# Hash-masked attention and gated feed-forward: the score scale moved into the query rows, and the exponential's factor and shift instructions removed

## The chip, the cores and the metric

The kernel runs on one core of a Trainium2 chip. The metric is the device time of one execution in microseconds, the median over runs. The engines are named as the profile names them: PE (matrix multiply, with PEld for its weight loads), DVE (vector), ACT (scalar, activation functions), POOL (GpSimd) and SP (whose queue issues almost all DMAs).

## The reference

The reference is an attention in which a query row sees only the keys that fall into the same hash bucket, followed by a gated feed-forward layer. Sizes: 4 batches, 8 heads, 768 positions, head size 64, 6 hash bits; all arithmetic is in float32.

```
q_bits = (einsum('bhsd,dk->bhsk', q, proj) > 0);  k_bits likewise
mask   = q_bucket[:, :, :, None] == k_bucket[:, :, None, :]
scores = (1 / sqrt(64)) * q @ k^T
scores = where(mask, scores, -1e9);  scores = scores - max(scores)
attn   = exp(scores);  attn = attn / (sum(attn) + 1e-09)
x      = attn @ v                      # heads side by side: 4 x 768 x 512
gate   = sigmoid(causal depthwise convolution of x, 5 taps)
out    = (gate * (x @ w_val)) @ w_out
```

A query row without any key in its bucket has the same score, -1e9, everywhere, so its weights are 1/768 each.

## The kernel before

There are 32 units (batch, head), and each has 6 tiles of 128 query rows by 768 keys: 192 tiles, numbered k. The queries and keys of a unit arrive transposed in one array `r` of 128 rows, queries in rows 0 to 63 and keys in rows 64 to 127. `prep` makes four operands of it, in a rounded and a remainder part, so that two passes of matmuls (`scores`, L266) give an accurate product: `aq`, `ak` (rounded; 12 further rows carry the hash bits, so that a mismatch adds a large negative number to the score) and `bq`, `bk` (remainders crossed with rounded parts). POOL makes the rounded copy (L170, `aq<-r`) and the remainder (L173, `bq<-r,aq`); six DMAs of SP (L174 to L177, L181, L182) then move the halves to where the matmul needs them, and L148 (`load_raw`) fetches the `r` of five units later. The operands exist twice (`stk`, two buffers), so the operands of unit i+1 are made while unit i is computed.

A tile runs through these steps. PE writes the scores `s` into one of two PSUM buffers. DVE takes the negated row maximum `nm` (L272). `factors` (L278, DVE) makes `gs`, which is the score scale 1/8 for an ordinary row and 0 for a row without a match; `shifts` (L282, DVE) makes `nb = nm * gs`. ACT computes `p = exp(gs * s + nb)` and the row sum (L290). For each pair of tiles, DVE adds 1e-9 to the sums (L296) and takes the reciprocal `ri` (L300); POOL multiplies `p` by it (L305). Three tiles later PE transposes `p` (L314), ACT copies the transposes out of PSUM (L323, `pt<-tp`), and PE multiplies them with the values (L337, `av`). ACT copies `av` to `x` (L345); DVE and POOL do the convolution (L366, L368), ACT the gate (L372), and PE the two feed-forward products (L399, L424). The 8 weight blocks come as 64-bit numbers and are turned into a rounded and a remainder part during the first quarter: a DMA on SP (L137), ACT's absolute value (L91), DVE and POOL operations (L93 to L113).

The order on PE, ACT, DVE and POOL is written out by hand: one loop over k (L490 and on) issues, for each k, the copies of tile k-4, the maximum of k, the sums of the pair before, the normalisation of k-2, `scores(k+1)`, the exponential of k, and one step each of the generators for convolutions, weights, feed-forward, `prep` and `attn_v`. A generator stops at each `yield` and goes on in a later iteration. `prep` of the next unit is created when k is the last tile of a unit (k = 5 modulo 6), gets its first step there and one step per tile after it; `finish(preps)` forces the rest before the first `scores` of the next unit. SP is not ordered by hand: a scheduler places its DMAs by its own estimate of when they become ready.

Of the kernel before, what the change touches and what calls it, by code (L numbers as in the profile page):

```python
# [8 lines left out]
FP32 = mybir.dt.float32  # L9
# [17 lines left out]
def kernel(  # L27
# [13 lines left out]
    D = 64  # L41
# [38 lines left out]
    cw_sb = const.tile([P, NP * KW], FP32, name="cw_sb")  # L80

# [79 lines left out]
    def prep(i):  # L161
# [8 lines left out]
        nc.gpsimd.tensor_copy(out=aq, in_=r)  # L170
        if i > 1:
            yield
        nc.gpsimd.tensor_tensor(out=bq, in0=r, in1=aq.bitcast(FP32), op=ALU.subtract)  # L173
# [64 lines left out]
    def first_prep():  # L238
# [7 lines left out]
        nc.scalar.copy(out=aq[0:D], in_=r[0:D])  # L246
# [3 lines left out]
        for g in (0, 2, 3, 1):  # L250
            if g == 1:
                nc.vector.tensor_tensor(out=bq[D:P], in0=r[0:D], in1=aq[0:D].bitcast(FP32), op=ALU.subtract)  # L252
# [4 lines left out]
        nc.scalar.copy(out=bq[0:D], in_=r[0:D])  # L257
# [11 lines left out]
    def maxima(k):  # L269
        s = ss[k]  # L270
        nm = small.tile([P, 1], FP32, name="nm")
        nc.vector.tensor_reduce(out=nm, in_=s[:, :, 0:HS], axis=AX.XY, op=ALU.max, negate=True)  # L272
        nms[k] = nm

    def factors(k):

        gs[k] = small.tile([P, 1], FP32, name="gs")
        nc.vector.tensor_scalar(out=gs[k], in0=nms[k], scalar1=BIG / 2, scalar2=scale, op0=ALU.is_lt, op1=ALU.mult)  # L278

    def shifts(k):  # L280
        nbs[k] = small.tile([P, 1], FP32, name="nb")
        nc.vector.tensor_scalar(out=nbs[k], in0=nms.pop(k), scalar1=gs[k], scalar2=None, op0=ALU.mult)  # L282

    def exponentials(k):
        s, nb = ss.pop(k), nbs.pop(k)
# [4 lines left out]
        nc.scalar.activation(out=p, in_=s[:, :, 0:HS], func=AF.Exp, bias=nb, scale=gs.pop(k), accum_out=sm[:, k % 2, 0:1])  # L290
        ps[k] = (p.rearrange("p a b -> p (a b)"), sm)


    def row_sums(k):
        sums[k] = small.tile([P, 2, 2], FP32, name="s1")
        nc.vector.tensor_scalar(out=sums[k][:, :, 0], in0=ps[k][1][:, :, 0], scalar1=1e-9, scalar2=None, op0=ALU.add)  # L296

    def recip(k):
        ri = small.tile([P, 2], FP32, name="ri")
        nc.vector.reciprocal(out=ri, in_=sums.pop(k)[:, :, 0])  # L300
        rcs[k], rcs[k + 1] = ri[:, 0:1], ri[:, 1:2]

    def normalise(k):
        p, _ = ps[k]
        nc.gpsimd.tensor_scalar(out=p, in0=p, scalar1=rcs.pop(k), scalar2=1.0, op0=ALU.mult, op1=ALU.mult)  # L305
# [170 lines left out]
    with tc.manual_schedule(engines=ENGINES):  # L476
# [13 lines left out]
        for k in range(N + LAG + 1):  # L490
# [5 lines left out]
            if pair:  # L496
                row_sums(k - 2)
# [100 lines left out]
```

## Time and profile before

| | |
|---|---|
| median of 3 runs | 621.8 us (621.5 to 622.37) |
| profiled execution, span from first to last instruction | 620.8 us |
| PE busy | 585.5 us, 94% of the span |
| DVE busy | 437.6 us, 70% |
| ACT busy | 421.4 us, 68% |
| POOL busy | 395.6 us, 64% |

The profile gives no other time for the profiled execution than its span; the median of the runs lies 1.0 us above it, the lowest run 0.7 and the highest 1.6. Share of busy time is an average over the whole execution: the first third, in which weights are prepared and the operands for later units are loaded, looks different from the rest, and the prediction reads the two apart.

### The profile page before, as it was taken

To read this page: it belongs to the slowest core of one execution; us is meant where nothing else is said; L and a number is where in the kernel's file an instruction comes from. 1 tells how busy PE (TensorE), PEld (TensorE's weight loads), DVE (VectorE), ACT (ScalarE), POOL (GpSimd) and SP (SyncE) were. 2 spreads that over 40 slices of the span, in tenths; PEclk is the share of its full clock that TensorE was granted. 3 is DMA by queue.
4 is the path that set the end of the run, shared out by engine and by line. 5 is a ranking of instruction groups with operands and counts; after the bars stand their busy time and mean duration, and the time that the engine had idled before them with its cause. 6 is when DMAs were issued, how large, how long until landed. Compare 5 with 4: busy or idle time off the path is not lost.

```text
span 620.8 us, 10648 instructions
## 1 busy us (share of the span) xinstructions
PE 585.5 (94%) x3496; PEld 423.4 (68%) x3496; DVE 437.6 (70%) x1017; ACT 421.4 (68%) x881; POOL 395.6 (64%) x373
## 2 busy tenths in 40 slices
PE   5789898989999999999999999999999999999997
PEld 2655565555657777776767777777667877775895
DVE  5869798998975866668575867569665877665532
ACT  2777777778778666777787676777787766765400
POOL 3576868778766765578564777568764777544321
PEclk9799999999999999999999999999999999999999
DMA  6467666564532235243433234333422213200111
GB/s 227 123 197 199 200 167 208 157 175 118 133 83 68 70 79 142 72 108 82 122 82 107 61 80 126 84 115 82 108 70 78 67 42 91 69 18 1 51 52 51
DMA packets 29031, 64.64 MB, mean 104 GB/s; under 512 B 4937, under 2 KB 10057, under 8 KB 28977
## 3 DMA queue, kind: packets, MB, share of 16 engines
q1 hardware_dynamic: 28832, 63.93, 37.8%
q8 instruction: 28, 0.46, 0.3%
q14 instruction: 27, 0.21, 0.1%
q10 hardware_dynamic: 144, 0.03, 0.0%
HBM read 30.60 MB, written 7.86 MB: 62 GB/s over the span
## 4 chain that ended last, share of the span: by engine, by line
PE 66%; DVE 12%; ACT 12%; DMA 5%; issue 3%; POOL 2%; SPq 1%; ACTq 0%; POOLq 0%; DVEq 0%
PE av L337 17%; PE s L266 16%; PE tp L314 12%; PE m L424 8%; PE m L399 7%; ACT p L290 5%; DVE nm L272 4%; ACT pt L323 3%; ACT x L345 2%; DMA w<-in_w_val_dram 2%; DVE g L368 2%; PE tp L399 1%; PE tp L424 1%; PE s L424 1%; DMA bk<-bq 1%
## 5 line engine op out<-in xcount | busy, mean ns | idle before, releaser
L305 POOL TENSOR_SCALAR p<-p,ri 128x768 f32<-128x768 f32 x192 | 210.5, 1100 | 156.0 <-DVE nb L282 130.8
L272 DVE TENSOR_REDUCE nm<-s 128x1 f32<-128x768 f32 x192 | 182.5, 950 | 61.2 <-PE s L266 61.0
L290 ACT ACTIVATE p<-s,nb,gs 128x768 f32<-128x768 f32 x192 | 192.6, 1003 | 46.2 <-DVE nb L282 41.9
L323 ACT COPY pt<-tp 128x384 f32<-128x384 f32 x384 | 165.7, 485 | 75.3 <-PE tp L314 74.4
L314 PEld LDWEIGHTS tp<-ident,p 128*128 128x128 f32 x1152 | 130.3, 142 | 72.2 <-issue 43.6
L314 PE MATMUL tp<-ident,p 128*128 128x128 f32 x1152 | 164.4, 279 | 2.6 <-ACT pt L323 2.1
L337 PE MATMUL av<-pt,vt 128*64 128x384 f32 x768 | 144.9, 498 | 0.0
L266 PE MATMUL s<-ak,aq 76*128 76x384 f32 x384 | 118.1, 389 | 23.2 <-ACT p L290 19.7
L266 PE MATMUL s<-bk,bq 128*128 128x384 f32 x384 | 101.3, 345 | 0.4 <-DVE bq L252 0.4
L337 PEld LDWEIGHTS av<-pt,vt 128*64 128x64 f32 x768 | 47.0, 136 | 61.5 <-issue 61.4
L266 PEld LDWEIGHTS s<-ak,aq 76*128 76x128 f32 x384 | 59.2, 194 | 38.7 <-ACT p L290 34.6
L368 DVE SCALAR_TENSOR_TENSOR g<-x,cw_sb,g 128x768 f32<-128x768 f32 x64 | 79.4, 1241 | 2.2 <-POOL g L366 2.1
L266 PEld LDWEIGHTS s<-bk,bq 128*128 128x128 f32 x384 | 71.7, 194 | 0.8 <-issue 0.8
L173 POOL TENSOR_TENSOR bq<-r,aq 128x768 fp32r<-128x768 f32 x31 | 59.2, 1909 | 0.1
L410 POOL TENSOR_TENSOR hl<-ht,hh 128x384 fp32r<-128x384 f32 x32 | 32.3, 1009 | 39.5 <-DVE hh L408 39.5
L345 ACT COPY x<-av 64x384 f32<-64x384 f32 x64 | 30.4, 475 | 29.7 <-PE av L337 29.0
L282 DVE TENSOR_SCALAR nb<-nm,gs 128x1 f32<-128x1 f32 x192 | 40.4, 211 | 3.5
L399 PE MATMUL m<-xh,wv 128*128 128x384 f32 x200 | 42.7, 337 | 0.0
L358 POOL TENSOR_TENSOR xl<-x,xh 128x384 fp32r<-128x384 f32 x32 | 33.4, 1059 | 13.8 <-DVE xh L357 13.8
L290 ACT ACTIVATION_READ_ACCUMULATOR p<-s,nb,gs 128x1 f32 x192 | 39.0, 203 | 0.0
L404 DVE TENSOR_TENSOR ht<-m,g 128x384 f32<-128x384 f32 x25 | 13.9, 556 | 35.6 <-PE m L399 29.2
L424 PE MATMUL m<-wo,hh 128*128 128x512 f32 x144 | 38.1, 394 | 0.0
(86 smaller groups left out, 486.9 us busy)
## 6 DMA issues: line engine op xcount, KB each, us to landing
r<-in_qk_dram SPq DMA_DIRECT2D x32, 384.0 KB
vt<-in_v_dram SPq DMA_DIRECT2D x16, 384.0 KB
out_dram<-o SPq DMA_DIRECT2D x24, 256.0 KB
ak<-aq SPq DMA_DIRECT2D x31, 192.0 KB
bk<-aq SPq DMA_DIRECT2D x31, 192.0 KB
bk<-bq SPq DMA_DIRECT2D x31, 192.0 KB
bq<-aq SPq DMA_DIRECT2D x31, 192.0 KB
hh<-in_qk_dram SPq DMA_DIRECT2D x16, 192.0 KB
```

The costliest lines, as they stand in the source:

```text
L173: nc.gpsimd.tensor_tensor(out=bq, in0=r, in1=aq.bitcast(FP32), op=ALU.subtract)
L266: nc.tensor.matmul(out=s[:, hf, 0:HS], lhsT=lq[0:n, qs], rhs=rk[0:n, hf * HS:(hf + 1) * HS], start=n == M, stop=n == P)
L272: nc.vector.tensor_reduce(out=nm, in_=s[:, :, 0:HS], axis=AX.XY, op=ALU.max, negate=True)
L290: nc.scalar.activation(out=p, in_=s[:, :, 0:HS], func=AF.Exp, bias=nb, scale=gs.pop(k), accum_out=sm[:, k % 2, 0:1])
L305: nc.gpsimd.tensor_scalar(out=p, in0=p, scalar1=rcs.pop(k), scalar2=1.0, op0=ALU.mult, op1=ALU.mult)
L314: nc.tensor.transpose(out=tp[:, n * P:(n + 1) * P], in_=p[:, kb * P:(kb + 1) * P], identity=ident)
L323: nc.scalar.copy(out=pt[:, :, qo:qo + P], in_=tp[:, 0:HS].rearrange("p (a b) -> p a b", b=P))
L337: nc.tensor.matmul(out=av[s * D:(s + 1) * D, 0:HS], lhsT=vt[:, kb, hh * D:(hh + 1) * D], rhs=pt[kb // 3][:, kb % 3, :], start=(kb == 0), s ...
L345: nc.scalar.copy(out=x[hh * D:(hh + 1) * D, o:o + HS], in_=av[s * D:(s + 1) * D, 0:HS])
L368: nc.vector.scalar_tensor_tensor(out=g, in0=x[:, k:k + S], scalar=w, in1=g, op0=ALU.mult, op1=ALU.add)
L399: nc.tensor.matmul(out=acc[:, 0:HS], lhsT=wv[wi][:, c, j * P:(j + 1) * P], rhs=xs_[(c, o)][xi], start=(m == 0), stop=(m == 11))
L424: nc.tensor.matmul(out=acc, lhsT=hs[(o, j)][hi][:, tb * P:(tb + 1) * P], rhs=wo[wi][:, j, :], start=(m == 0), stop=(m == 11))
```

## The change

The score scale, 1/8, goes into the query rows. For units 2 to 31, `prep` gets a new first step, an activation on ACT that multiplies rows 0 to 63 of `r` by the scale in place; the rounded copy on POOL and the remainder with the DMAs behind it each come one step later than before. For unit 1 the scale is part of the two operations that make `aq` and `bq` (a per-row factor `shrink`), and the remainder is made on DVE; for unit 0 it is part of operations that were there already. The exponential then needs no factor: its scale is 1.0 and its bias is `nm` itself, so `factors` and `shifts` are gone. A row without a match is set right later: `unmatched` makes, once per pair of tiles, `fs`, which holds (1, 768) for such a row and (0, 0) for any other; the row sum becomes `max(sum + 1e-9, fs[1])`, and the normalisation on POOL becomes `max(p, fs[0]) * ri`.

```
         r = raws[i]
         aq, ak, bq, bk = stacks[i] = [...]
-        nc.gpsimd.tensor_copy(out=aq, in_=r)
         if i > 1:
-            yield
-        nc.gpsimd.tensor_tensor(out=bq, in0=r, in1=aq.bitcast(FP32), op=ALU.subtract)
+            nc.scalar.activation(out=r[0:D], in_=r[0:D], func=AF.Copy, scale=scale)
+            yield
+            nc.gpsimd.tensor_copy(out=aq, in_=r)
+            yield
+            nc.gpsimd.tensor_tensor(out=bq, in0=r, in1=aq.bitcast(FP32), op=ALU.subtract)
+        else:
+            nc.gpsimd.tensor_scalar(out=aq, in0=r, scalar1=shrink, scalar2=1.0, op0=ALU.mult, op1=ALU.mult)
+            nc.vector.scalar_tensor_tensor(out=bq, in0=r, scalar=shrink, in1=aq.bitcast(FP32),
+                                           op0=ALU.mult, op1=ALU.subtract)
...
-        nc.vector.tensor_scalar(out=gs[k], in0=nms[k], scalar1=BIG / 2, scalar2=scale, op0=ALU.is_lt, op1=ALU.mult)
-        nc.vector.tensor_scalar(out=nbs[k], in0=nms.pop(k), scalar1=gs[k], scalar2=None, op0=ALU.mult)
...
-        nc.scalar.activation(out=p, in_=s[:, :, 0:HS], func=AF.Exp, bias=nb, scale=gs.pop(k), accum_out=sm[:, k % 2, 0:1])
+        nc.scalar.activation(out=p, in_=s[:, :, 0:HS], func=AF.Exp, bias=nms.pop(k), scale=1.0, accum_out=sm[:, k % 2, 0:1])
...
+    def unmatched(k):
+        fs[k] = small.tile([P, 2, 2], FP32, name="fs")
+        nc.vector.scalar_tensor_tensor(out=fs[k], in0=pairs.pop(k).unsqueeze(2).to_broadcast([P, 2, 2]), scalar=BIG / 2,
+                                       in1=alone, op0=ALU.is_ge, op1=ALU.mult)
     def row_sums(k):
-        nc.vector.tensor_scalar(out=sums[k][:, :, 0], in0=ps[k][1][:, :, 0], scalar1=1e-9, scalar2=None, op0=ALU.add)
+        nc.vector.scalar_tensor_tensor(out=sums[k], in0=ps[k][1][:, :, 0], scalar=1e-9, in1=fs[k][:, :, 1],
+                                       op0=ALU.add, op1=ALU.max)
...
-        nc.gpsimd.tensor_scalar(out=p, in0=p, scalar1=rcs.pop(k), scalar2=1.0, op0=ALU.mult, op1=ALU.mult)
+        nc.gpsimd.tensor_scalar(out=p, in0=p, scalar1=f, scalar2=ri, op0=ALU.max, op1=ALU.mult)
```

How the rows stand now on three engines. First DVE, two consecutive tiles between the fifth and the sixth weight block (`nm`, `gs`, `nb`: the maximum, factor and shift of one tile; `s_1397` and `ri`: sums and reciprocals of the pair before; `g`, `xh`: convolution), of which the second tile is even; before:

```order
L272 TENSOR_REDUCE nm<-s 128x1
L278 TENSOR_SCALAR gs<-nm 128x1
L282 TENSOR_SCALAR nb<-nm,gs 128x1
L368 SCALAR_TENSOR_TENSOR g<-x,cw_sb,g 128x768
L357 CAST xh<-x 128x384 x2
L272 TENSOR_REDUCE nm<-s 128x1
L296 TENSOR_SCALAR s_1397<-sm 128x2
L278 TENSOR_SCALAR gs<-nm 128x1
L300 RECIPROCAL ri<-s_1397 128x2
L282 TENSOR_SCALAR nb<-nm,gs 128x1
```

The same place on DVE now (line numbers are higher by the added lines):

```order
L287 TENSOR_REDUCE nm<-s 128x1
L383 SCALAR_TENSOR_TENSOR g<-x,cw_sb,g 128x768
L372 CAST xh<-x 128x384 x2
L287 TENSOR_REDUCE nm<-s 128x1
L303 SCALAR_TENSOR_TENSOR fs<-nm,alone 128x4
L308 SCALAR_TENSOR_TENSOR s_1289<-sm,fs 128x2
L313 RECIPROCAL ri<-s_1289 128x2
```

An odd tile has lost two small instructions and gained none; an even tile has lost two and gained one, and its three small instructions now form a chain, `fs` to `s` to `ri`.

Next POOL, where the operands of unit 5 are made (`wv`: the end of a weight block); before:

```order
L305 TENSOR_SCALAR p<-p,ri 128x768
L113 TENSOR_TENSOR wv_121<-w_527 128x512
L170 CAST aq<-r 128x768
L305 TENSOR_SCALAR p<-p,ri 128x768
L173 TENSOR_TENSOR bq<-r,aq 128x768
```

Unit 5 on POOL now:

```order
L119 TENSOR_TENSOR wv_127<-w_490 128x512
L320 TENSOR_SCALAR p<-p,fs,ri 128x768
L179 CAST aq<-r 128x768
L320 TENSOR_SCALAR p<-p,fs,ri 128x768
L381 TENSOR_SCALAR g<-x,cw_sb 128x768
L181 TENSOR_TENSOR bq<-r,aq 128x768
```

The copy and the remainder each stand one normalisation later, and here the convolution's first tap (`g`) has come in front of the remainder too; in even-numbered units it has not.

Last SP, the end of the DMAs of unit 6, with the sixth weight block behind them; before:

```order
L176 DMA bk<-bq 64x768
L181 DMA aq<-u 12x768
L154 DMA vt<-in_v_dram 128x768
L177 DMA bq<-aq 64x768
L148 DMA r<-in_qk_dram 128x768
L137 DMA w_1333<-in_w_out_dram 128x1024
```

The same place on SP now:

```order
L188 DMA bk<-bq 64x768
L193 DMA aq<-u 12x768
L154 DMA r<-in_qk_dram 128x768
L189 DMA bq<-aq 64x768
L143 DMA w_1228<-in_w_out_dram 128x1024
```

The weight block still stands behind the whole group, whose first DMA here waits for POOL's remainder; the values (`vt`) have gone ahead of that first DMA.

More of the change, by code (lines that the diff above doesn't have):

```diff
@@ L80 @@
     cw_sb = const.tile([P, NP * KW], FP32, name="cw_sb")
+    shrink = const.tile([P, 1], FP32, name="shrink")
+    nc.gpsimd.memset(shrink[0:D], scale)
+    nc.gpsimd.memset(shrink[D:P], 1.0)
+    alone = const.tile([P, 2, 2], FP32, name="alone")
+    nc.gpsimd.memset(alone[:, :, 0], 1.0)
+    nc.gpsimd.memset(alone[:, :, 1], float(S))
     wv = [const.tile([P, NP, 512], FP32R, name=f"wv{i}") for i in range(2)]
@@ L245, in first_prep @@
                              rhs=r[:, HS * (g % 2):HS * (g % 2 + 1)], start=True, stop=True, tile_position=(0, 32 * g))
-        nc.scalar.copy(out=aq[0:D], in_=r[0:D])
+        nc.scalar.activation(out=aq[0:D], in_=r[0:D], func=AF.Copy, scale=scale)
         nc.vector.tensor_copy(out=bk[D:P], in_=r[D:P])
@@ L251, in first_prep @@
             if g == 1:
-                nc.vector.tensor_tensor(out=bq[D:P], in0=r[0:D], in1=aq[0:D].bitcast(FP32), op=ALU.subtract)
+                nc.vector.scalar_tensor_tensor(out=bq[D:P], in0=r[0:D], scalar=scale, in1=aq[0:D].bitcast(FP32),
+                                               op0=ALU.mult, op1=ALU.subtract)
             nc.vector.tensor_scalar(out=(aq, ak)[g // 2][D:M, HS * (g % 2):HS * (g % 2 + 1)],
@@ L256, in first_prep @@
                                     scalar2=rows_sb[32 * g:32 * g + 2 * NB, 3:4], op0=ALU.is_ge, op1=ALU.mult)
-        nc.scalar.copy(out=bq[0:D], in_=r[0:D])
+        nc.scalar.activation(out=bq[0:D], in_=r[0:D], func=AF.Copy, scale=scale)
     def scores(k):
@@ L270, in maxima @@
         s = ss[k]
[L271 to L282, printed above, removed]
+        if k % 2 == 0:
+            cur["nm"] = small.tile([P, 2], FP32, name="nm")
+        nms[k] = cur["nm"][:, k % 2:k % 2 + 1]
+        nc.vector.tensor_reduce(out=nms[k], in_=s[:, :, 0:HS], axis=AX.XY, op=ALU.max, negate=True)
+        if k % 2:
+            pairs[k - 1] = cur["nm"]
     def exponentials(k):
-        s, nb = ss.pop(k), nbs.pop(k)
+        s = ss.pop(k)
         p = pp.tile([P, 2, HS], FP32, name="p")
@@ L456 @@
     tiles = [(i, qt) for i in range(len(units)) for qt in range(KB)]
-    raws, stacks, vts, ss, nbs, ps, tps, sums, rcs, nms, gs, cur = {}, {}, {}, {}, {}, {}, {}, {}, {}, {}, {}, {}
+    raws, stacks, vts, ss, ps, tps, sums, rcs, nms, pairs, fs, cur = {}, {}, {}, {}, {}, {}, {}, {}, {}, {}, {}, {}
     avs, convs, moes, early = [], [], [], {}
@@ L496 @@
             if pair:
+                unmatched(k - 2)
                 row_sums(k - 2)
-            if k < N:
-                factors(k)
-            if pair:
                 recip(k - 2)
@@ L503 @@
                 normalise(k - 2)
-            if k < N:
-                shifts(k)
             if k + 1 < N:
```

8 lines of the change are left out of this document (5 added, 3 removed).

## The prediction

> **What bounds the kernel now.** I read four views: the busy time of each engine by stage, the waits by stage, the chain of work that ended last, and the groups of instructions. First the page's span and the stages; the columns are the stretch, its length, then the busy time of PE, PEld, DVE, ACT and POOL.
>
> ```profile
> span 620.8 us, 10648 instructions
> 10.00:200.00 190.00, 170.84 (x1054) 111.71 (x1053) 160.01 (x374) 141.75 (x297) 135.64 (x124) 0.98 0.55 150
> 200.00:565.00 365.00, 360.79 (x2180) 269.14 (x2179) 251.28 (x603) 266.75 (x563) 240.22 (x227) 1.00 0.32 84
> ```
>
> From 200 to 565 us PE is busy for 360.8 of 365.0 us: 4.2 us are to be had there, whatever DVE, ACT or POOL save. From 10 to 200 us PE is idle for 19.2 us. That is where the change can pay, and 19.2 + 4.2 = 23.4 us is the most that it can bring there. Next, the waits of the first stage (in total, times, longest), then one of the second:
>
> ```profile
> ACT p L290 <- DVE nb L282: 26.5, 31, 6.0
> PE s L266 <- ACT p L290: 16.9, 24, 1.8
> DVE nm L272 <- PE s L266: 7.3, 9, 1.6
> ACT o L91 <- DMA w<-in_w_val_dram: 3.3, 2, 1.7
> ```
>
> ```profile
> PE s L266 <- ACT p L290: 2.8, 8, 0.4
> ```
>
> In the first stage nearly all of PE's idle time, 16.9 us in 24 waits, is `scores(k+1)` waiting until the exponential of k-1 has freed its PSUM buffer, and ACT in its turn waits for `nb` 31 times, 26.5 us. DVE waits for PE only 7.3 us: it is the engine that sets the pace, and the chain shows how. Columns are start, duration, engine:
>
> ```profile
> 88.63 0.87 DVE nm L272
> ...
> 89.53 0.17 DVE gs L278
> ...
> 89.72 0.21 DVE nb L282
> 89.93 1.28 DVE g L368
> ...
> 91.81 0.87 DVE nm L272
> 92.68 0.07 DVE s L296
> 92.76 0.11 DVE gs L278
> 92.87 0.09 DVE ri L300
> 92.96 0.16 DVE nb L282
> ```
>
> The maximum of an odd tile ends at 89.50 and `nb` at 89.93, so `gs` and `nb` take 0.43 us there; in the even tile the four small instructions take 93.12 - 92.68 = 0.44 us. In both, the exponential and everything behind it on DVE stand behind them.
>
> **The change part by part.** Groups of the whole execution (form, count, busy time, mean ns), and the pairs of tiles in the first stage by the group of their sums there:
>
> ```profile
> L290 ACT ACTIVATE p<-s,nb,gs 128x768 f32<-128x768 f32 x192 | 192.6, 1003 | 46.2 <-DVE nb L282 41.9
> L372 ACT ACTIVATE g<-g 128x768 f32<-128x768 f32 x16 | 12.2, 833 | 0.0
> L246 ACT CAST aq<-r 64x768 fp32r<-64x768 f32 x1 | 0.8, 832 | 1.9 <-DMA r<-in_qk_dram 1.9
> L170 POOL CAST aq<-r 128x768 fp32r<-128x768 f32 x31 | 28.7, 925 | 0.4 <-PE s L266 0.3
> L305 POOL TENSOR_SCALAR p<-p,ri 128x768 f32<-128x768 f32 x192 | 210.5, 1100 | 156.0 <-DVE nb L282 130.8
> L366 POOL TENSOR_SCALAR g<-x,cw_sb 128x768 f32<-128x768 f32 x16 | 15.0, 939 | 0.0
> L296 DVE TENSOR_SCALAR s<-sm 128x2 f32<-128x2 f32 x34 | 5.6, 166 | 1.2 <-ACT p L290 1.2
> ```
>
> *Shorter way from the maximum to the exponential.* Every exponential starts 0.43 to 0.44 us earlier behind its maximum. It also gets shorter: of its two per-row operands (`nb`, `gs`) one is left. The trace has no exponential with one; the bounds are 1003 ns (L290, two) and 833 ns (L372, same shape, none). I take the middle, 0.09 us less. So each of the 24 waits can shrink by 0.44 + 0.09 = 0.53 us, 12.7 us in all. But they average 16.9 / 24 = 0.70 us, some are shorter than 0.53, and some end with something other than `nb`. I take three quarters: **-9.5 us**. From 200 us on only the 0.09 counts, for 8 waits: **-0.7 us**.
>
> The Trainium skill ("ScalarE: Activation LUTs", section "What ACT_TABLE_LOAD costs") says that each per-partition pointer operand of an activation adds about 93 ns. By it the term would be an estimated 0.44 + 0.093 per wait, which moves the sum by less than 0.1 us; no row here shows an activation with just one.
>
> *DVE's own time.* An odd tile loses 0.43 us. An even tile loses `gs` and `nb` and gains `fs`, and `fs`, `s` and `ri` now wait for each other. I count 0.10 for `fs` (its input is old, like the row of `s` above, 0.07) and 0.2 each for `s` and `ri` (like `gs` and `nb` behind the maximum of the odd tile, 0.17 to 0.21 plus a gap of 0.02): 0.5 instead of 0.44. So a pair saves 0.43 - 0.06 = 0.37 us, and the 34 pairs of the first stage 12.6 us. This is the same money seen from the other side, not a further term: it says that 9.5 us can be paid without DVE becoming late again.
>
> *The new step on ACT.* It has the size of L246: 832 ns, for 30 units 25 us. It stands behind the exponential of an odd tile. What covers it later on is this idle time (start, duration, what, idle before):
>
> ```profile
> 312.62 0.19 ACT L290 ACTIVATION_READ_ACCUMULATOR p<-s,nb,gs 128x1 f32 x1
> 313.99 0.86 ACT L323 COPY pt<-tp 128x384 f32<-128x384 f32 x2 [1.19 <-PE tp L314]
> ```
>
> 1.19 us before the next copies hide 0.83 us; without them it would cost 0.83 us per unit. In the first stage, ten units, ACT's wait for `nb` is the cover (26.5 / 31 = 0.85 us each), and the change takes half of that away. Between nothing and 10 x 0.83 = 8.3 us I take **+1.5 us**.
>
> *Later operands.* POOL's remainder now comes behind one more normalisation and the copy: 1.10 + 0.93 = 2.0 us later, and where `g` has slipped in front (about every second unit) another 0.94. Its DMAs move with it. How much room is there? Unit 2 is the tightest that I found (start and duration of the issue; start of the first matmul that reads it; then one such transfer with the releases around it, in another unit):
>
> ```profile
> 33.39 0.48 SPq L177 DMA_DIRECT2D bq<-aq  x1
> 38.66 0.51 PE L266 MATMUL s<-bk,bq 128*128 128x384 f32 x2
> ```
>
> ```profile
> 60.54 2.27 POOL bq L173
> 62.82 2.53 DMA bk<-bq
> 65.37 0.51 SPq L177
> ...
> 66.55 6.39 DMA w<-in_w_val_dram
> ```
>
> A transfer of this size takes 2.53 us; 38.66 - 33.39 - 2.53 = 2.7 us are to spare, and a shift of 2.0 to 2.9 with an earlier next unit uses them up. Most units have more, so I take half a microsecond for three units of the first stage: **+1.5 us** (between 0 and 31 x 0.5 = 15.5).
>
> The same rows hold the weights: the DMA `w` sits on SP behind the whole group, so it too is issued 2 us later, while ACT's L91 stands where it stood. Before, ACT waited like this:
>
> ```profile
> 72.96 0.70 ACT L91 ACTIVATE o<-w 128x512 f32<-128x512 f32 x1 [1.67 <-DMA w<-in_w_val_dram]
> 105.92 0.67 ACT L91 ACTIVATE o<-w 128x512 f32<-128x512 f32 x1 [0.53 <-DMA w<-in_w_out_dram]
> ```
>
> Behind the waiting L91 are queued the copies of transposes and the next exponential, for which PE waits. Three weight blocks (the fourth, sixth and eighth) stand behind such a group: 3 x 2.0 = 6.0 us more of ACT's waiting at most, nothing at least if PE has work meanwhile. I take **+3.5 us**. The second block is now ahead of its group, and its wait (3.3 - 1.67 = 1.6 us) goes; I take about two thirds of that as what PE lost: **-1.0 us**.
>
> *Edits at no cost.* The normalisation with `max` and a second per-row operand: L366 and L305 do 768 numbers with one operand, the copy L170 with none, and the three rows lie between 925 and 1100 ns; POOL has 190 - 136 = 54 us idle in the first stage, so a tenth of a microsecond more on 69 normalisations is hidden; without that cover it would cost 7 us. The constants, unit 0 and unit 1: single instructions at the start, in the cover of the first loads.
>
> The sum: -9.5 - 0.7 - 1.0 + 1.5 + 1.5 + 3.5 = **-4.7 us**, 616.1 us of span. With the 1.0 us between span and median of the runs, 617.1; I say **617.0 us**. A measurement of this kernel can tell about 0.2% (1.2 us) from no change.
>
> **The rivals.**
>
> *All of it lands.* If the DMAs' room suffices and PE works through ACT's waits, only the gains stay: -9.5 - 0.7 - 1.0 = -11.2, 610.6 us. For it: most units have more room than unit 2. Against it: L91 waited already. Chance 0.25.
>
> *The small instructions fight POOL.* `fs` and the new `s` read two tensors from SBUF where `gs`, `nb` and the old `s` read one. The trace shows what that can mean (start, duration):
>
> ```profile
> 311.52 1.04 DVE L368 SCALAR_TENSOR_TENSOR g<-x,cw_sb,g 128x768 f32<-128x768 f32 x1
> 315.54 1.82 POOL L173 TENSOR_TENSOR bq<-r,aq 128x768 fp32r<-128x768 f32 x1
> 316.34 1.84 DVE L368 SCALAR_TENSOR_TENSOR g<-x,cw_sb,g 128x768 f32<-128x768 f32 x1
> 22.38 2.17 POOL L305 TENSOR_SCALAR p<-p,ri 128x768 f32<-128x768 f32 x2 [2.51 <-DVE nb L282]
> 23.69 0.16 DVE L97 SCALAR_TENSOR_TENSOR cw<-cw,cwt 128x20 int32<-128x20 int32 x1
> ```
>
> The same instruction took 1.04 us and, under POOL's remainder, 1.84 us. At that ratio 0.2 us become 0.35, and 2 x 34 of them 10 us, all that the first stage gains: with the costs, 620.8 + 0.5 + 1.0 = 622 us. Against it: L97, a small one of this kind, took 0.16 us while POOL was normalising. Chance 0.05. The Trainium skill says this ("GPSIMD Engine Reference", section "Key points"): POOL shares its SBUF interfaces with the vector engine, and instructions of that engine with two SBUF inputs contend. The L368 rows agree; the L97 row does not show it for a small one.
>
> *The handover becomes the bound.* Slower than before: the operands of each next unit arrive after the first `scores` that needs them. The place is the first `bk,bq` matmul of a unit, the price what the shift (2.0, in every second unit 2.9) exceeds the room by. It decides from (4.7 / 31) = 0.15 us per unit on, beyond what I have counted; at 0.4 us per unit it is 620.8 - 4.7 + 12.4 = 628.5, 629.5 us in the runs, at half that 623. For it: DMAs wait in line on SP, each for the one before. Against it: 2.7 us of room in the tightest unit. Chance 0.15.
>
> *Nothing comes of it.* What is late next on PE's side, the copies of transposes in front of the exponential on ACT, is late by nearly as much: 621.8 us. Chance 0.10.
>
> **How the numbers follow.** The forecast has 0.45, the rivals 0.25, 0.05, 0.15 and 0.10. The first two cases cover 609.5 to 620, from all gains with 1 us of error to the forecast's costs nearly doubled; with the case of no effect and the near end of the slower ones up to 622.5 they hold 0.8. Faster by over 0.2%: 0.45 + 0.25 and 0.03 of the case of no effect, 0.73. Slower: 0.15, and 0.02 each of contention and no effect, 0.19. Within: the rest, 0.08.
>
> **What would show it.** Right: the waits of ACT for the maximum, in the first stage, well under the 26.5 us for `nb`; PE's idle time there down from 19.2 to about 14; the exponential near 910 ns; ACT's waits for `w` longer, two or three of 2 to 4 us. Wrong: an exponential still near 1000 ns; a normalisation well over 1.2 us, which would make POOL the bound; first `scores` of units waiting for DMAs by more than a few tenths; `fs` and `s` over 0.3 us; or a stage after 200 us whose PE idle time grows beyond 4.2 us because the new step on ACT is not covered.

## The result, and the profile after

The change makes the kernel slower: 825.86 us against 622.09 us in the same comparison, a ratio of 1.327 [1.324, 1.329]. The forecast was 617.0 us, faster, with 622.5 as the upper end. First the page of the profiled execution: its span, the busy time of the engines, POOL's share and the granted clock of TensorE in 40 slices, and the chain of work that ended last.

```profile
span 823.9 us, 10497 instructions
PE 650.2 (79%) x3496; PEld 451.7 (55%) x3496; DVE 426.7 (52%) x730; ACT 428.0 (52%) x911; POOL 759.1 (92%) x376
POOL 3999999989999999999999999999999999999521
PEclk9689798878887999998897999999998999998899
POOL 50%; PE 25%; issue 15%; DVE 6%; DMA 2%; ACT 1%; POOLq 0%; DVEq 0%; SPq 0%; ACTq 0%
```

Before, POOL was busy for 395.6 us, PE for 94% of the span. Now POOL is busy for 759.1 us, its row of tenths stands at 9 in all but one slice from the second to the 37th (a 9 is 90% or more), and half of the chain runs through it. DVE and ACT, for whose sake the change was made, hardly differ. The same page says which group it is (busy, mean ns of one, idle before and its releaser):

```profile
L320 POOL TENSOR_SCALAR p<-p,fs,ri 128x768 f32<-128x768 f32 x192 | 581.4, 3034 | 19.0 <-DVE cwt L99 9.4
L329 PE MATMUL tp<-ident,p 128*128 128x128 f32 x1152 | 184.3, 301 | 157.2 <-POOL p L320 154.6
L297 ACT ACTIVATE p<-s,nm 128x768 f32<-128x768 f32 x192 | 175.5, 914 | 23.8 <-DVE nm L287 17.2
```

The normalisation takes 3034 ns where it took 1100. That is 192 x 1.93 = 371 us more work for POOL. Before, POOL was idle for 620.8 - 395.6 = 225 us; now it is idle for 823.9 - 759.1 = 65 us. POOL's busy time grew by 363.5 us in all (its other instructions got a little shorter or fewer); 160 us of that fitted into the idle time, and the other 203 us are what the span grew by. The third line shows that the exponential did become shorter, 914 ns for 1003; the forecast said near 910.

The waits (in total, times, longest) show who stands behind POOL, and the stages (length, then busy PE, PEld, DVE, ACT, POOL; then the granted clock) show that it does so from start to end:

```profile
ACT pt L338 <- PE tp L329: 279.8, 166, 5.1
PEld tp L329 <- POOL p L320: 227.7, 135, 4.0
PE tp L329 <- POOL p L320: 154.6, 100, 3.7
```

```profile
10.00:200.00 190.00, 139.85 (x720) 88.48 (x719) 116.83 (x199) 98.32 (x214) 180.15 (x83) 0.82 0.44 123
200.00:565.00 365.00, 291.94 (x1614) 203.96 (x1614) 182.43 (x317) 206.58 (x441) 359.17 (x173) 0.93 0.27 69
```

The transposes wait for the normalised tile 100 times, 154.6 us, a wait that was not among the large ones before. In the second stage, where PE was busy for 360.8 of 365.0 us, POOL is now, for 359.2. The clock column fell too, to 0.82 and 0.93.

### The profile page after: what moved, and what is told of

Same layout as the page of the kernel before. It is cut to its first block, busy times and chain, and to the rows that moved or that the text cites. A ratio compares the mean times of both kernels' runs of the same rounds, so it can differ in the third digit from the quotient of the medians.

```text
span 823.9 us, 10497 instructions
## 1 busy us (share of the span) xinstructions
PE 650.2 (79%) x3496; PEld 451.7 (55%) x3496; DVE 426.7 (52%) x730; ACT 428.0 (52%) x911; POOL 759.1 (92%) x376
## 4 chain that ended last, share of the span: by engine, by line
POOL 50%; PE 25%; issue 15%; DVE 6%; DMA 2%; ACT 1%; POOLq 0%; DVEq 0%; SPq 0%; ACTq 0%
POOL p L320 34%; PE tp L329 6%; POOL bq L181 6%; PE s L279 5%; PE av L352 4%; POOL xl L373 3%; PE m L439 3%; POOL hl L425 2%; POOL aq L179 2%; DVE nm L287 2%; PE m L414 2%; POOL g L381 1%; PE tp L414 1%; PE tp L439 1%; POOL w L117 1%
## 5 line engine op out<-in xcount | busy, mean ns | idle before, releaser
L320 POOL TENSOR_SCALAR p<-p,fs,ri 128x768 f32<-128x768 f32 x192 | 581.4, 3034 | 19.0 <-DVE cwt L99 9.4
L329 PE MATMUL tp<-ident,p 128*128 128x128 f32 x1152 | 184.3, 301 | 157.2 <-POOL p L320 154.6
L329 PEld LDWEIGHTS tp<-ident,p 128*128 128x128 f32 x1152 | 137.4, 152 | 255.7 <-POOL p L320 227.7
L297 ACT ACTIVATE p<-s,nm 128x768 f32<-128x768 f32 x192 | 175.5, 914 | 23.8 <-DVE nm L287 17.2
L352 PE MATMUL av<-pt,vt 128*64 128x384 f32 x768 | 165.9, 560 | 0.0
L279 PE MATMUL s<-ak,aq 76*128 76x384 f32 x384 | 125.3, 410 | 5.5 <-ACT p L297 3.8
L383 DVE SCALAR_TENSOR_TENSOR g<-x,cw_sb,g 128x768 f32<-128x768 f32 x64 | 87.8, 1372 | 79.2 <-POOL g L381 79.0
L279 PE MATMUL s<-bk,bq 128*128 128x384 f32 x384 | 108.5, 367 | 0.4 <-DVE bq L264 0.4
L297 ACT ACTIVATION_READ_ACCUMULATOR p<-s,nm 128x1 f32 x192 | 39.9, 208 | 0.0
L308 DVE SCALAR_TENSOR_TENSOR s<-sm,fs 128x2 f32<-128x2 f32 x96 | 32.0, 334 | 10.8 <-ACT p L297 1.0
```

Source lines behind the costliest of these rows:

```text
L279: nc.tensor.matmul(out=s[:, hf, 0:HS], lhsT=lq[0:n, qs], rhs=rk[0:n, hf * HS:(hf + 1) * HS], start=n == M, stop=n == P)
L320: nc.gpsimd.tensor_scalar(out=p, in0=p, scalar1=f, scalar2=ri, op0=ALU.max, op1=ALU.mult)
L329: nc.tensor.transpose(out=tp[:, n * P:(n + 1) * P], in_=p[:, kb * P:(kb + 1) * P], identity=ident)
L352: nc.tensor.matmul(out=av[s * D:(s + 1) * D, 0:HS], lhsT=vt[:, kb, hh * D:(hh + 1) * D], rhs=pt[kb // 3][:, kb % 3, :], start=(kb == 0), s ...
L383: nc.vector.scalar_tensor_tensor(out=g, in0=x[:, k:k + S], scalar=w, in1=g, op0=ALU.mult, op1=ALU.add)
```

## Experiments: what made it slower

The theory after the result: one of the two things that are new in the normalisation, `max` or the second per-row operand, is slow on POOL. The rival: the rest of the change, by holding up the tiles, lets POOL's instructions wait inside their own duration.

**The maximum alone.** The kernel before, with one edit:

```
-        nc.gpsimd.tensor_scalar(out=p, in0=p, scalar1=rcs.pop(k), scalar2=1.0, op0=ALU.mult, op1=ALU.mult)
+        nc.gpsimd.tensor_scalar(out=p, in0=p, scalar1=0.0, scalar2=rcs.pop(k), op0=ALU.max, op1=ALU.mult)
```

> The kernel before, with POOL's normalisation as max(p, 0) * ri: the maximum is there, with a constant, and only ri is read per row. If it is the maximum that POOL is slow at, one normalisation takes about 2.9 us as in the changed kernel (1.1 before) and the time is 810 to 840 us. If it is the second per-row operand, the normalisation stays at 1.1 us and the time at 622 us. If only the two together are slow, also 622 us.

808.98 us, ratio 1.297 [1.293, 1.300]. POOL's group:

```profile
L305 POOL TENSOR_SCALAR p<-p,ri 128x768 f32<-128x768 f32 x192 | 564.4, 2946 | 17.3 <-DVE nb L282 16.9 <-PE tp L314 0.4
```

With nothing else changed, a maximum with 0 in the place of a product with 1.0 is worth 186 of the 204 us (808.98 against 622.86 us in this comparison; 810 to 840 was expected). The rest is near what the second operand costs once POOL is the bound, an estimate: (3034 - 2946) x 192 = 17 us.

**The second operand alone.** The kernel before with `p * ri * one`, where `one` is a second per-row operand that holds 1.0.

> The kernel before, with the normalisation as p * ri * one, where one is a column of ones: no maximum, two per-row operands. If the second per-row operand is what is slow, 2.9 us a piece and over 800 us in all; if it is the maximum, 1.0 to 1.2 us a piece and 622 us, within 0.3%.

623.71 us, ratio 1.0008 [0.9993, 1.0024].

```profile
L307 POOL TENSOR_SCALAR p<-p,ri,one 128x768 f32<-128x768 f32 x192 | 227.3, 1187 | 139.7 <-DVE nb L284 118.1 <-PE tp L316 16.3 <-ACT pt L325 2.5
```

1187 ns for 1100: a second per-row operand costs 0.09 us, and here, where POOL has idle time, that is hidden, as the forecast had it.

**The change without the maximum.** The changed kernel with the normalisation of before, `p * ri * 1.0`; everything else is the change.

> The changed kernel with the normalisation as it was before (p * ri, no maximum; left out: the weights of rows without a match, which are then not uniform). This is the rest of the change alone. If the slow normalisation is the whole loss, and the forecast's other terms hold, 617 us (609.5 to 622.5), with the normalisation at 1.1 us. If the later operands or the new step on ACT cost more than forecast, 623 to 630 us. If the loss is not POOL's, over 650 us.

624.88 us, ratio 1.0024 [1.0003, 1.0045].

```profile
L320 POOL TENSOR_SCALAR p<-p,ri 128x768 f32<-128x768 f32 x192 | 202.2, 1057 | 177.0 <-DVE ri L313 96.7 <-PE tp L329 41.3 <-ACT r L177 10.8
```

The normalisation takes 1057 ns. The rest of the change makes nothing slower by much. But it does not make the kernel faster either: +2.0 us where the forecast's sum is -4.7.

**Another way to set the rows right.** The changed kernel with a product and a sum in the normalisation, which gives the same output: `fs` holds (1/768, BIG) for a row without a match, so that `p * ri` is next to nothing there and 1/768 is added.

```
-        nc.gpsimd.tensor_scalar(out=p, in0=p, scalar1=f, scalar2=ri, op0=ALU.max, op1=ALU.mult)
+        nc.gpsimd.tensor_scalar(out=p, in0=p, scalar1=ri, scalar2=f, op0=ALU.mult, op1=ALU.add)
```

> The changed kernel with rows without a match set right by an addition in place of the maximum: p * ri + c, where such a row gets ri near 0 and c = 1/768, any other c = 0. Two per-row operands, two different operations, no maximum. If the maximum is what is slow: the normalisation at 1.0 to 1.2 us and the same time as the kernel without the maximum, within 2 us. If POOL is slow at any pair of different operations, or at two per-row operands, 2.9 us a piece and over 800 us.

626.72 us, ratio 1.0058 [1.0041, 1.0075].

```profile
L320 POOL TENSOR_SCALAR p<-p,ri,fs 128x768 f32<-128x768 f32 x192 | 221.5, 1156 | 160.1 <-DVE ri L313 93.4 <-PE tp L329 32.1 <-DVE cwt L99 8.8
```

The normalisation takes 1156 ns with its two operands. So the idea of the change can be had without the slow operation, at +3.9 us.

**Which operations, and by what they cost.** The kernel before with six forms of the normalisation by turns, all with the same output.

> The kernel before with six forms of the normalisation by turns, one per tile of a unit, all with the same output: a product and a product; a product and a maximum with 0; a minimum with 2 and a product; a sum with 0 and a product; a maximum with 0 and a product on two halves of 384 numbers; the same on 768. If maximum and minimum are slow on GpSimd wherever they stand and by the element: about 2.9 us for the second, third and sixth form, twice 1.5 us for the halves, 1.1 us for the first and fourth. If only a first operation that is no product is slow: 1.1 us for the second, 2.9 us for the fourth. If the cost is one fixed time per instruction: twice 2.5 us for the halves. About 700 us in all.

754.91 us in its one run, where about 700 was expected. The groups, in the order halves with `max` first; `max` first; `mult` then `max`; `min` first; `add` first; two products:

```profile
L315 POOL TENSOR_SCALAR p<-p,ri 128x384 f32<-128x384 f32 x64 | 115.6, 1813 | 31.6 <-DVE nb L282 31.6
L317 POOL TENSOR_SCALAR p<-p,ri 128x768 f32<-128x768 f32 x32 | 94.1, 2939 | 0.0
L307 POOL TENSOR_SCALAR p<-p,ri 128x768 f32<-128x768 f32 x32 | 93.8, 2930 | 0.0
L309 POOL TENSOR_SCALAR p<-p,ri 128x768 f32<-128x768 f32 x32 | 92.8, 2900 | 17.3 <-DVE nb L282 14.8 <-PE tp L328 2.1 <-ACT pt L337 0.4
L311 POOL TENSOR_SCALAR p<-p,ri 128x768 f32<-128x768 f32 x32 | 30.9, 966 | 0.0
L319 POOL TENSOR_SCALAR p<-p,ri 128x768 f32<-128x768 f32 x32 | 29.8, 930 | 7.4 <-DVE nb L282 6.5 <-PE tp L328 0.8
```

Maximum and minimum, first or second, take 2.90 to 2.94 us; sum and product 0.93 to 0.97, as expected; a half takes 1.81, where 1.5 was expected. The halves say that it goes by the number: (2939 - 1813) / 384 = 2.93 ns for each and, if a straight line joins the two lengths, 0.69 us that does not depend on it. It is the maximum, not the second operand; and since the kernel before slows down by the maximum alone, the rival is out.

## Experiments: where the forecast gain went

Left open was why the rest gives +2.0 or +3.9 us and not -4.7. Three theories: the operands that come later and the new step on ACT cost more than the forecast gave them; the small instructions with two tensors wait for POOL; or the shorter way was never worth 9.5 us.

**Step and lateness together.** The kernel before, with the copy of the query rows onto themselves as a new first step of `prep` and everything behind it a step later.

```
+        if i > 1:
+            nc.scalar.activation(out=r[0:D], in_=r[0:D], func=AF.Copy, scale=1.0)
+            yield
         nc.gpsimd.tensor_copy(out=aq, in_=r)
```

> The kernel before with one thing added: the first step of a unit's preparation copies the 64 query rows onto themselves on ScalarE (times 1.0), and the cast, the remainder and the transfers come one step later. Factors, shifts and the normalisation are those of before. If the later operands and the new step are what takes the gain away: the forecast's terms +1.5, +1.5, +3.5 and -1.0 make +5.5 us, 628 us; ScalarE's waits for the fourth, sixth and eighth weight block 0.8 to 1.8 us longer than before. If they cost nothing, because PE has other work meanwhile: 622 to 624 us.

635.61 us, ratio 1.0202 [1.0187, 1.0216]: +12.9 us, against +5.5 (628 us) by the forecast's terms.

**The step alone.** The kernel before, with the step on ACT at the end of the unit before (behind `load_raw(i + 5)`, on `raws[i + 1]`), so that nothing is late.

> The kernel before with only ScalarE's step on the query rows (times 1.0), at the end of the unit before, so that the cast, the remainder and the transfers stay where they were. Of the 12.9 us that step and lateness cost together: if the step on ScalarE is the larger part, 630 us or more; if it is the size that the forecast gave it, +1.5, about 624 us.

625.82 us, ratio 1.0037 [1.0020, 1.0053]: +3.2 us. Its group:

```profile
L186 ACT ACTIVATE r<-r 64x768 f32<-64x768 f32 x30 | 25.0, 833 | 0.0
```

833 ns as the forecast had it from L246. What it costs is twice the +1.5 between the medians; the interval of the ratio, +1.2 to +3.3 us, does not exclude the +1.5.

**Lateness alone.** The kernel before with one `yield` more ahead of the copy, and no step on ACT.

> The kernel before with only the lateness: the cast, the remainder, the transfers and the hash bits of the next four units come one step later, and ScalarE has no new step. If lateness is the larger part of the 12.9 us: 630 to 636 us. If it is the size that the forecast gave it, +1.5 +3.5 -1.0 = +4.0, about 627 us. If it costs nothing without the step on ScalarE: 623 us.

631.31 us, ratio 1.0135 [1.0115, 1.0155]: +8.7 us, against +4.0. Waits of PE in the first stage:

```profile
PE s L268 <- ACT p L292: 20.9, 32, 1.5
PE m L228 <- DVE u L209: 2.5, 2, 1.7
```

PE's wait for exponentials grew from 16.9 to 20.9 us, and there is a new one, for `u`. The forecast had not seen that `bits(i + 1)`, the hash projections of the next four units, hangs on the same generator: the extra `yield` moves it too, into the turn in which `early_bits` wants the one buffer `m`.

**Lateness without the hash bits.** The same with `bits` back at its old steps.

```
-                yield
                 yield from bits(i + 1)
```

> The kernel with only the lateness (631.3 us, 8.7 more than before), with the hash bits of the next four units back at their old steps; the cast, the remainder and the transfers stay one step late. If PE's projections of the bits, which met the early projections at the one buffer m and waited 0.8 and 1.7 us for u, are a large part of the 8.7: 628 us or less. If they are no more than the waits that the trace shows: about 629 us. If they cost nothing beside the rest: 631 us.

627.40 us, ratio 1.0081 [1.0068, 1.0093]: +5.4 us, and the new wait is nearly gone:

```profile
PE m L205 <- DVE u L208: 0.4, 1, 0.4
```

So about 3 of the 8.7 us belong to the hash bits, and some 5.4 to the operands, copies and loads.

**The weight blocks' waits.** The kernel of the run before, and the kernel before the change, each with one `yield` more between the load of a weight block and ACT's first work on it.

> The kernel before this one in the list, with one step more between the load of a weight block and ScalarE's first work on it, so that ScalarE has no wait for the fourth, sixth and eighth block (2.0, 1.0 and 1.7 us with the lateness alone). If these waits, with the copies and exponentials queued behind them, are what lateness costs: 3 to 5 us less than without the step. If not: the same within 1 us, and the cost lies in the operands of the units themselves.

> The kernel before with the same one step more between the load of a weight block and ScalarE's work on it, nothing late: what the step itself does. Its waits for the second, fourth and sixth block (1.6, 1.7 and 0.5 us) go. If they were on the way, 1 to 3 us less than before, about 620.5 us; if the weights' work only meets other work a step later: 622 to 625 us.

629.89 us, ratio 1.0123 [1.0110, 1.0136], with lateness; 626.26 us, ratio 1.0062 [1.0046, 1.0077], without. Both are slower for the step, where 3 to 5 us less or no change, and 620.5 to 625 us, were expected. The step costs 4.3 us by itself and 2.5 us where the waits were longer, so these waits are worth perhaps 2 us in the late kernel. That is inside what the step itself disturbs, and how the 5.4 us are shared out stays open.

**Rows scaled early.** The kernel with product and sum (626.72 us), with the query rows of unit i+1 scaled at the end of `prep(i)`. Nothing is late.

> The changed kernel with the product and sum in the normalisation, and with the query rows of the next unit scaled at the end of this unit's preparation, so that the cast, the remainder and all transfers stand at the steps of the kernel before. If the later operands took the gain away: 626.7 - 5.5 = 621 us or less, the weight blocks' waits of ScalarE as in the kernel before, no wait of PE's hash projections for u beyond half a microsecond. If the lateness cost nothing: 625 to 628 us, as the kernel with the rows scaled late.

622.65 us, ratio 1.0001 [0.9986, 1.0015]: some 4 us less than with the late rows, but no gain over before; 621 us or less was expected if lateness had taken the gain. The timeline shows what else is in the way (start, duration, engine; `x2` is two instructions shown as one):

```profile
61.27 1.01 POOL L320 TENSOR_SCALAR p<-p,ri,fs 128x768 f32<-128x768 f32 x1
...
61.59 0.69 DVE L308 SCALAR_TENSOR_TENSOR s<-sm,fs 128x2 f32<-128x2 f32 x1 [0.18 <-ACT p L297]
...
65.94 2.00 POOL L373 TENSOR_TENSOR xl<-x,xh 128x384 fp32r<-128x384 f32 x2 [0.30 <-DVE xh L372]
...
67.01 0.95 DVE L303 SCALAR_TENSOR_TENSOR fs<-nm,alone 128x4 f32<-128x4 f32 x1
68.06 0.16 DVE L308 SCALAR_TENSOR_TENSOR s<-sm,fs 128x2 f32<-128x2 f32 x1
```

`s` starts under a normalisation and ends when that ends, at 62.28; `fs` starts under `xl` and ends when that ends, at 67.94 to 67.96. Where POOL is idle, `s` takes 0.16 us. These two do not share POOL's time, they wait for its instruction to end. They are no exceptions: of the 96 `s` of this trace 29 take 0.57 to 0.86 us and the rest 0.16, of the 96 `fs` 19 take 0.32 to 1.02, and every one of these 48 ends within 0.1 us of the end of an instruction of POOL.

**One tensor each.** The same kernel, with `fs` and `s` replaced by instructions that read one tensor.

```
-        nc.vector.scalar_tensor_tensor(out=fs[k], in0=pairs.pop(k)..., scalar=BIG / 2, in1=alone, op0=ALU.is_ge, op1=ALU.mult)
-        nc.vector.scalar_tensor_tensor(out=sums[k], in0=ps[k][1][:, :, 0], scalar=1e-9, in1=fs[k][:, :, 1], ...)
+        nc.vector.tensor_scalar(out=sm[:, :, 1], in0=nm, scalar1=BIG / 2, scalar2=BIG, op0=ALU.is_ge, op1=ALU.mult)
+        nc.vector.tensor_scalar(out=fs[k], in0=nm, scalar1=BIG / 2, scalar2=1.0 / S, op0=ALU.is_ge, op1=ALU.mult)
+        nc.vector.tensor_reduce(out=sums[k], in_=ps[k][1], axis=AX.X, op=ALU.add)
```

> The kernel with the rows scaled early, and every small instruction of VectorE that sets the rows without a match right now reads one tensor: two comparisons of the negated maxima (one written beside the sums), and the row sums by a reduction over the two columns, in the place of fs and s with two tensors each. If small two-tensor instructions wait for GpSimd's running instruction (fs and s up to 1.0 us instead of 0.15) and this is on the way: none of the four above 0.25 us, and 622.7 - 3 = about 620 us or less. If that waiting is in VectorE's idle time: 622 to 624 us, the one instruction more paid for or hidden.

617.97 us, ratio 0.9929 [0.9903, 0.9955]: 4.6 us faster than before, and the fastest kernel here. First the two groups of the kernel before this edit, then those that replace them:

```profile
L308 DVE SCALAR_TENSOR_TENSOR s<-sm,fs 128x2 f32<-128x2 f32 x96 | 32.7, 341 | 10.9 <-ACT p L297 0.9 <-DVE fs L303 0.5
L303 DVE SCALAR_TENSOR_TENSOR fs<-nm,alone 128x4 f32<-128x4 f32 x96 | 25.4, 264 | 0.0
```

```profile
L303 DVE TENSOR_SCALAR sm<-nm 128x2 f32<-128x2 f32 x96 | 25.0, 260 | 0.0
L305 DVE TENSOR_SCALAR fs<-nm 128x2 f32<-128x2 f32 x96 | 17.2, 179 | 0.0
...
L309 DVE TENSOR_REDUCE s<-sm 128x2 f32<-128x4 f32 x96 | 15.0, 156 | 4.2
```

The sum `s` falls from 341 to 156 ns; the first instruction behind the maximum, `sm`, still takes 260, which was not expected. It reads one tensor and waits all the same (start, duration; POOL's instruction ends at 112.05, `sm` at 112.08):

```profile
110.23 1.82 POOL L179 TENSOR_TENSOR bq<-r,aq 128x768 fp32r<-128x768 f32 x1
111.05 1.03 DVE L303 TENSOR_SCALAR sm<-nm 128x2 f32<-128x2 f32 x1
```

Of the 96 `sm` 19 take more than 0.3 us, and each ends with an instruction of POOL. So the number of tensors is not what decides. None of the 96 new `s` (a reduction) and none of the reciprocals `ri` takes longer than 0.17 us, though more than a fifth of them run from start to end under an instruction of POOL. Together the three take 57 us, the two before took 58. What changed is which of them is long: `s` stands between the exponential and `ri`, for which POOL waits. That the 4.6 us come from there is argued from these rows; that the exchange of the instructions is worth them is measured.

PE's wait for exponentials in the first stage, which the forecast wanted to shorten, fell with it (16.9 us in 24 waits before):

```profile
PE s L279 <- ACT p L297: 11.9, 25, 1.7
```

**The exponential's way alone.** Operands and `prep` of before; the exponential takes the constant 0.125 as its scale and `nb`, one product of the maximum, as its bias. Once with the two-tensor `fs` and `s`, once with one tensor each.

> The preparation of the operands is that of the kernel before (rows not scaled, no step on ScalarE, nothing later). The exponential takes the constant 0.125 as its scale and, as its bias, the negated maximum times 0.125, one instruction on VectorE right behind the maximum; rows without a match are set right by a product and a sum in the normalisation. If the way from the maximum to the exponential is worth what the forecast gave it, and the later operands took it away: 24 waits x 0.4 us x three quarters + 0.7 us = 8 us less than before, about 615 us. If the gain of that way was never there, because ScalarE's copies of the transposes and PE's own work are late next: 621 to 623 us. If the small instructions of VectorE that read two tensors take it back behind GpSimd: 624 to 626 us, as in the two kernels with the scaled rows, with fs and s at 0.28 to 0.33 us on average.

> The kernel with the operands of before and the exponential's way alone, with the same one-tensor form. It took 627.5 us with two-tensor fs and s. If their waiting for GpSimd is what made it slower than the kernel before: below 623 us, near 618. If something else did (slow stretches of PE's clock, the product and sum in the normalisation): 626 to 628 us again.

627.52 us, ratio 1.0071 [1.0059, 1.0083], and 623.91 us, ratio 1.0025 [1.0012, 1.0038]. The one-tensor form is worth 3.6 us here, 4.7 above. Both runs missed: without the step on ACT and without lateness, 615 to 618 us was expected if the way was worth what the forecast gave it, and neither came out at the other times named. PE's wait for exponentials in the first stage is 18.6 and 17.5 us in them, no shorter than the 16.9 before.

**The way, or the number of instructions.** What the last kernel has and the fastest has not is `nb` between maximum and exponential. The fastest kernel, once with two idle products per pair behind `ri`, once with two in the way (each tile's `nm` times 1.0 as the bias).

> The fastest kernel so far (rows scaled early, small instructions with one tensor: 618.0 us, 4.6 less than before) with two idle products of one number per row added on VectorE for each pair of tiles, behind the reciprocal, that nobody reads. Six small instructions per pair then, as in the kernel before, but none of the new ones between a maximum and its exponential. If the gain comes from the shorter way between these two, as the forecast worked it out: 618 to 619 us. If it comes from the number of VectorE's small instructions (0.15 us each and a gap): 620.5 to 622.5 us.

> The same kernel with the two added products in the way: each tile's negated maximum is multiplied by 1.0 by an instruction of its own and the exponential takes that as its bias, 0.25 us later behind its maximum. If the way is what counts: 30 such delays x 0.25 us x three quarters = 5.6 us and 22 turns after 200 us with nearly nothing, about 623.5 us. If the number of instructions counts: as the kernel with the two products behind the reciprocal, within 1 us.

619.70 us, ratio 0.9952 [0.9934, 0.9970], and 626.50 us, ratio 1.0079 [1.0058, 1.0099]. Against 617.97 us the same instructions cost 1.7 us behind the reciprocal, which lies within the intervals, and 8.5 us in the way, where 5.6 was expected (behind it, 618 to 619 us was expected if the way counts, 620.5 to 622.5 if the number does). So what counts is the place between maximum and exponential; the number of instructions is the smaller part. That the gain of the fastest kernel is the shorter way's, as the forecast had it, fits this but is not shown by it. The kernel with two in the way is 4.2 us slower than the one before the change, although one small instruction stands in its way (154 ns) and two stood there before, and its exponential is shorter too; the kernel with the exponential's way alone, with one there as well, is no faster than before either. Why is open. Three rows of the first stage, of the fastest kernel, of the one with two behind, and of the one with two in the way:

```profile
10.00:200.00 190.00, 174.75 (x1064) 113.46 (x1063) 159.14 (x306) 144.20 (x312) 143.21 (x124) 0.99 0.56 153
```

```profile
10.00:200.00 190.00, 170.67 (x1050) 110.44 (x1051) 164.25 (x368) 142.83 (x309) 144.14 (x123) 0.98 0.55 150
```

```profile
10.00:200.00 190.00, 171.51 (x1029) 110.77 (x1028) 167.05 (x363) 138.80 (x301) 133.88 (x119) 0.95 0.56 150
```

PE's idle time is 15.3, 19.3 and 18.5 us, before 19.2. It does not tell the last two apart, although they differ by 6.8 us, nor does PE's wait for exponentials (15.0 and 15.8 us). The clock column does in these two executions: 0.98 and 0.95 over 190 us are 3.8 and 9.5 us of lost PE time. But the clock is not what separates the two kernels. The three runs of the one with two in the way that had a mean clock of 0.992 to 0.993 took 625.9 to 626.4 us, the four of the one with two behind at 0.991 to 0.994 took 619.4 to 621.1. The last section comes back to this.

## Why the prediction was wrong

**The step that failed** is the one under "Edits at no cost": "The normalisation with `max` and a second per-row operand: L366 and L305 do 768 numbers with one operand, the copy L170 with none, and the three rows lie between 925 and 1100 ns". All three rows are products or copies. They bound what a further operand costs, and that held (0.09 us). They say nothing of a maximum, and no row of before has POOL computing one on a tile. The bound was drawn from rows of the same shape, when what changed was the operation. It measured +1.9 us on 192 instructions, where "a tenth of a microsecond" was set in and 7 us "without that cover" was the worst that was named.

What could have been seen blind is the price at which it decides: POOL had 225 us idle, 225 / 192 = 1.17 us more for each normalisation, so near 2.3 us a piece it has no idle time left. An unknown operation on the engine whose one large group it is, 192 times, with no row, deserved a rival with that threshold. The forecast had named the sign ("a normalisation well over 1.2 us, which would make POOL the bound") and given it no chance.

**The shorter exponential**, -0.7 from 200 us on: its size was right, 914 ns, forecast near 910. After 200 us the fastest kernel gained more than the term said. The first exponential of unit 11 and the last of unit 31 (start, duration), in the kernel before and in the fastest:

```profile
195.98 0.99 ACT L290 ACTIVATE p<-s,nb,gs 128x768 f32<-128x768 f32 x1
...
562.26 0.99 ACT L290 ACTIVATE p<-s,nb,gs 128x768 f32<-128x768 f32 x1 [0.79 <-DVE nb L282]
```

```profile
194.53 0.90 ACT L297 ACTIVATE p<-s,nm 128x768 f32<-128x768 f32 x1
...
558.74 0.90 ACT L297 ACTIVATE p<-s,nm 128x768 f32<-128x768 f32 x1 [0.35 <-DVE nm L287]
```

The fastest kernel is 1.45 us ahead at the first place and 3.52 at the second: 2.1 us gained in between, where the forecast has 0.7. This is one execution of each, and how much of it is the exponential's and how much the shorter way's was not separated.

**The shorter way**, -9.5: the mechanism is borne out in part, and the size was too large for what was built on it. PE's wait for exponentials fell by 5.0 us (16.9 to 11.9) in the fastest kernel, and ACT's wait for the maximum from 26.5 to 18.6. This kernel is 4.6 us under before although it carries a step on ACT that costs 3.2 us in the kernel before; if the two add, way and exponential are worth some 7.8 us together, where the terms say 10.2. Two products put back into the way cost 8.5 us. Against it stands the kernel with the exponential's way alone, which is no faster than before.

**The new step on ACT**, +1.5: +3.2 us between the medians, an interval of +1.2 to +3.3; too small by up to a factor of two.

**Later operands and weight blocks**, +1.5 +3.5 -1.0: mis-sized, +8.7 us in the kernel before. An instruction had been left out: `bits` moves with the generator, and that is about 3 us. In the changed kernel, with a product and a sum in the normalisation, the same lateness costs some 4 us (626.72 against 622.65). The pieces do not simply add: -7.8 + 3.2 + 8.7 + 4.7 for the two-tensor instructions would be +8.8, and the kernel with all of them measured +3.9.

**The rival "small instructions fight POOL"** got 0.05 and was real: 3.6 and 4.7 us. It was priced as a ratio, 0.2 to 0.35 us; the `s` that wait take 0.57 to 0.86. It was set aside on the one row L97, which took 0.16 us under a normalisation. One fast row does not show that an instruction never waits: in the runs the small ones take 0.15 us or up to 1 us, by what POOL happens to run. Why L97 did not wait was not tried. The Trainium skill ("GPSIMD Engine Reference", section "Key points") had the rule, and the rows of `s` and `fs` above bear it out for instructions of 2 and 4 numbers. The page names a two-port mode of DVE beside two inputs from SBUF; whether that is why the one-tensor `sm` waits no run tried.

**The rival "the handover becomes the bound"** with 623 to 629.5 us is near what the change does once the maximum is gone (624.9 to 626.7), but that is luck, since its place is not the one: in the first stage of these two kernels the `scores` wait for transfers only 0.5 and 1.9 us, and PE's new wait for the hash bits `u` is larger (3.0 and 3.3 us).

## What to carry to other kernels

A cost is bounded by rows with the same operation on the same engine, not by rows of the same shape; where there is none, work out from the engine's idle time at which price it becomes the bound, and give that a chance. When a step of a generator is moved, list all that the same generator still issues. Small instructions of DVE on the way to a hand-over are to be timed one by one where POOL is busy beside them, by their longest and not by one row: here the two-tensor forms waited for POOL's instruction to end, and so did a one-tensor comparison, but a reduction and a reciprocal did not.

## What the runs showed of the hardware

**Maximum and minimum on POOL.** In a TENSOR_SCALAR instruction on 128 x 768 floats they take 2.90 to 2.95 us (3.03 with a second per-row operand). The run with six forms has the maximum in either place of the two, and in it two products take 0.93 us, a sum and a product 0.97; in the other kernels the forms without a maximum take 1.06 to 1.19. The Trainium skill ("GPSIMD Engine Reference", section "4.1 Engine selection") names max beside add and mul, with about line rate for one input. For product and sum the trace agrees (930 and 966 ns, where DVE's maximum over 768 numbers per row takes 950); for max it does not (2939 ns).

**PE's clock has stretches of some microseconds at half rate.** The kernel before shows one in its first stage (length, PE busy, ..., the granted clock is the third column from the end):

```profile
16.00:18.90 2.90, 0.96 (x4) 0.64 (x4) 2.78 (x8) 1.28 (x3) 0.82 (x1) 1.00 0.50 143
18.90:25.60 6.70, 6.30 (x24) 6.11 (x25) 5.86 (x16) 5.20 (x12) 3.91 (x5) 0.50 0.51 155
```

PE was busy for 0.96 of 2.90 us, and then ran 6.7 us at half clock, which is 3.35 us of its time. The kernel with the exponential's way alone, in its two-tensor form, has two such stretches:

```profile
26.90:33.60 6.70, 6.24 (x23) 5.64 (x24) 5.45 (x12) 4.24 (x11) 5.69 (x5) 0.50 0.39 98
95.30:102.00 6.70, 6.54 (x21) 4.12 (x22) 5.46 (x10) 3.88 (x11) 5.76 (x5) 0.50 0.75 218
```

The fastest kernel has one of 3.3 us. In the three microseconds before these three, PE was busy for 1.7, 1.2 and 1.2 us. But such waits do not always bring one; the kernel before, at another place:

```profile
125.80:128.70 2.90, 1.06 (x9) 0.79 (x8) 2.87 (x8) 1.30 (x4) 1.28 (x2) 1.00 0.65 139
128.70:135.40 6.70, 6.40 (x42) 3.82 (x42) 6.33 (x16) 5.27 (x12) 6.15 (x5) 1.00 0.52 142
```

The Trainium skill ("TensorE: Matmul & The Clock Gate", section "What's actually happening") has an activity window of about 3.4 us behind this; the stretches here are near one or two of these. Its table lets the clock fall after an idle window; here PE was not idle but busy for a third of the time before the fall, so the trace does not agree with that to the letter.

How much of the times is the clock's? Within one kernel a lower mean clock goes with a longer time: in the comparison with the first experiments the kernel before took 624.4 to 624.6 us in its three runs at 0.985, and 621.2 and 620.9 in those at 0.996 and 0.997. Between kernels it is the smaller part where runs of nearly the same clock can be compared. The two kernels with two products more stay some 5 to 7 us apart, of 6.8 (above). The exponential's way alone in its two-tensor form took 626.5 to 627.5 us at 0.986, the kernel before in that comparison 624.0 and 624.6 at 0.985, so 2 to 3.5 of its 4.8 us are left. Lateness alone costs 8.7 us, and in its profiled execution the clock was 1.00 throughout the first stage. So some short waits of PE can be paid twice, by some 3 us, but what makes these kernels slower than the ones beside them lies for the larger part elsewhere; for the first two it stays open. That the clock is a cause of the differences within a kernel, and does not only go along with one, was not tried.
